# A weight slab moved between DMA queues, ahead of a transposing load, and second-layer weights in one load fewer

## The chip, the core and the metric

The kernel runs on one core of one Trainium2 chip. The metric is the device time of one execution in microseconds (us): the median of the runs, with the lowest and highest beside it. A core has five engines that each follow their own instruction stream: TensorE (PE in the profile, with its weight loads listed apart as PEld), VectorE (DVE), ScalarE (ACT), GpSimd (POOL) and SyncE (SP). DMA transfers are issued by an engine's queue; in this kernel only SP and ScalarE issue any. Each issue costs the issuing queue some time, and the data land later.

## The reference

The kernel computes two branches from one input x of 2048 rows and 512 columns in bf16 and mixes them by a gate for each row.

```python
g = _sigmoid((x * gate_w).sum(-1, keepdims=True))
# branch A: linear attention, 32 heads of 16
qkv = x @ wqkv                        # split into q, k, v for each head
pq, pk = q @ w_phi, k @ w_phi         # for each head
phi_q = concat([softmax(pq), softmax(-pq)])
phi_k = concat([softmax(pk), softmax(-pk)])
kv = einsum("bhsf,bhsd->bhfd", phi_k, v)
z  = einsum("bhsf->bhf", phi_k)
o  = (phi_q @ kv) / (phi_q @ z + 1e-6)
a  = o @ wo
# branch B: dense layer, relu, dense layer; 512 -> 1376 -> 512
b  = relu(x @ w1) @ w2
out = g * a + (1 - g) * b
```

## The kernel before

The work is written out by hand in one order for each engine. A small planner collects the operations of each engine in program order, with the events that each waits for, and emits them; it does not reorder. `p.early` places what follows ahead of the program's opening barrier, so that SP and ScalarE begin to issue loads at the start of the span.

Matrix products want x with its columns on the 128 partitions, so x is held transposed in XT: four blocks of 128 columns, 2048 rows each. Rows are taken in four chunks of 512. For chunk 0, the first two column blocks are loaded plainly (L158), transposed on TensorE against an identity (L236) and evicted by VectorE and ScalarE (L246, L248). The other two blocks of chunk 0 come by a transposing DMA straight from memory (L174, event `x0t`). Chunks 1 to 3 come whole by transposing DMAs (L187).

The first layer's weights lie in W1, one slab of 128 input rows for each column block of x. Each slab's first 1024 columns are one load, but for slab 0, which has two. The remaining columns of all slabs are a load of their own (L177). TensorE multiplies slab by slab for chunk 0 (L519): slab t is eight matmuls, one into each of the eight PSUM banks, which accumulate over the four slabs. Slab 2 and slab 3 need the blocks of x that the transposing DMA brings:

```python
XV = (("xva0", "xvc0", "xvd0"), ("xva1",), ("x0t",), ("x0t",))
...
after=["w10a" if t == 0 and u < 4 else f"w1{t}", *XV[t]] + (free[UB[u]] if t == 0 else []),
```

SP's queue issues in this order: the two plain x loads, slab 0 in two, slab 1, the transposing load of x (`x0t`), slab 3, the remaining columns, the per-head weights (L179), the value weights (L181), the query and key weights by two transposing loads (L184, `wqk0` and `wqk1`), and chunks 1, 2 and 3 of x (L187). Slab 2 is issued by ScalarE, after ScalarE's second eviction of transposed x (L537 calls L162).

After the slabs, TensorE does the last two units of chunk 0 (L271), the gate column (L223), two value tiles (L403), and then folds the per-head weights into the query and key weights (L305): four groups that read `wqk0`, one value tile, four groups that read `wqk1`. The leftover hidden columns of chunk 0 follow (L283), and then the main loop of 16 row tiles: query and key products (L327), exponentials (L347), sums, reciprocals and products for the softmaxes, transposes of the features by DMA on SP (L396), the sum over rows (L425), value tiles, and first-layer units of the later chunks (L271). In row tile 3, SP loads the second layer's weights into W2, in three loads of 4, 3 and 3 row blocks and one of the last 96 rows (L584, L587). After the loop come the attention outputs (L457), the second layer (L482), the output projection (L491), the mix (L505) and the stores (L510). The second layer waits for all loads of W2.

Of the kernel before, what the change touches and what calls it, by code (L numbers as in the profile page):

```python
# [68 lines left out]
def bass_gated_mix__linear_kernel_hedgehog__dense_activation_relu__prompt_kernel(  # L69
# [16 lines left out]
    DFF = B_w1.shape[1]  # L86
    P = 128
# [14 lines left out]
    KU = KT - 1  # L102
    NR = DFF - KU * P

    with ExitStack() as es:
# [45 lines left out]
        p = _Plan(["sp", "pool", "act", "dve", "pe"])  # L151
# [6 lines left out]
            p.dma("sp", lambda e: e.dma_start(  # L158
                out=XS[:, 2 * h:2 * h + 2, 0:2 * P], in_=xq[:, 2 * h:2 * h + 2, 0:2 * P]), f"x0{h}", ev=f"x0{h}")

        def loadw1(t, c0=0, c1=DFF, tag="", eng="sp"):
            p.dma(eng, lambda e: e.dma_start(  # L162
                out=W1[:, t, c0:c1], in_=B_w1[t * P:(t + 1) * P, c0:c1]), f"w1{t}{tag}", ev=f"w1{t}{tag}")

        for h in range(2):
# [3 lines left out]
        p.early("act")  # L169
        p.early("sp")  # L170
        loadw1(0, 0, 4 * P, "a")
        loadw1(0, 4 * P, 8 * P)
        loadw1(1, 0, 8 * P)
        p.dma("sp", lambda e: e.dma_start_transpose(  # L174
            out=XT[:, 2:4, 0:512], in_=x2[0:512, 2 * P:4 * P]), "x0t", ev="x0t")
        loadw1(3, 0, 8 * P)
# [51 lines left out]
        def warm(n, cols=512):  # L228
            for _ in range(n):
                p.op("pe", lambda e: e.matmul(PS[:, 4, 0:cols], ones[:, 0:P], ones[:, 0:cols], start=True, stop=True),  # L230
                     after=["one"])
# [9 lines left out]
        def xev(eng, nm, js, dts, bank):  # L241
            w = len(js) * P
            d = XT[:, dts[0]:dts[-1] + 1, js[0] * P:js[0] * P + w]
            s = PS[:, bank, 0:len(dts) * w].rearrange("p (t c) -> p t c", c=w)
            if eng == "dve":
                p.op("dve", lambda e: e.tensor_copy(d, s), after=[f"xt{nm}"], ev=f"xv{nm}")  # L246
            else:
                p.op("act", lambda e: e.activation(d, s, ACT.Copy), after=[f"xt{nm}"], ev=f"xv{nm}")  # L248
            free[bank] = [f"xv{nm}"]
# [150 lines left out]
        def vtile(m, eng="act", bank=2):  # L400
            b = m % VB
            for dt in range(NDT):
                p.op("pe", lambda e, dt=dt: e.matmul(  # L403
                    PS[:, bank, :], XT[:, dt, m * P:(m + 1) * P], WV[:, dt, :],
                    start=(dt == 0), stop=(dt == NDT - 1)),
                    after=((xready(m // 4) + ["wv"] + free[bank]) if dt == 0 else ()),
                    ev=(f"v{m}" if dt == NDT - 1 else None))
            dst, src = VS[:, b, :, 0:64], PS[:, bank, :].rearrange("p (g c) -> p g c", g=NG)
            after = [f"v{m}"] + ([f"kv{m - VB}"] if m >= VB else [])
            if eng == "dve":  # L410
                p.op("dve", lambda e: e.tensor_copy(dst, src), after=after, ev=f"cv{m}")
            else:
                p.op("act", lambda e: e.activation(dst, src, ACT.Copy), after=after, ev=f"cv{m}")  # L413
            free[bank] = [f"cv{m}"]

        def kv(m):
            b = m % NB
            vb = m % VB
            for g in range(NG):
                after = []  # L420
                if g == 0:
                    after = [f"pk{m}", f"cv{m}", f"one{vb}"]
                    if m == 0:
                        after += free[6] + free[7]
                p.op("pe", lambda e, g=g: e.matmul(  # L425
                    PS[:, 6 + g // 4, (g % 4) * GW:(g % 4) * GW + 65],
                    EB[:, b, 3, g * P:(g + 1) * P], VS[:, vb, g, 0:65],
                    start=(m == 0 and g % 4 == 0), stop=(m == NT - 1), skip_group_check=True),
                    after=after, ev=(f"kv{m}" if g == NG - 1 else None))
# [104 lines left out]
        xev("act", "c0", (2,), (0,), 2)  # L534
        xev("dve", "d0", (3,), (0,), 1)
        xev("act", "a1", (0, 1, 2, 3), (1,), 7)
        loadw1(2, 0, 8 * P, eng="act")  # L537
        warm(1, 384)
        slab(0)
        for b in range(VB):  # L540
# [27 lines left out]
        def unit(c, k):  # L568
            if k < 0:
                rest(c)  # L570
            else:
                hunit(c, k)

        for m in range(NT):
            atile(m)
            if m >= LAG:
                kv(m - LAG)
            if m + 3 < NT:
                vtile(m + 3)
            for u in mid[m]:  # L580
                unit(*u)
            if m == 3:
                for a, b in ((0, 4), (4, 7), (7, KU)):
                    p.dma("sp", lambda e, a=a, b=b: e.dma_start(  # L584
                        out=W2[:, a:b, :], in_=B_w2[a * P:b * P, :].rearrange("(j p) n -> p j n", p=P)),
                        "w2", ev=f"w2{a}")
                p.dma("sp", lambda e: e.dma_start(out=W2[0:NR, KU, :], in_=B_w2[KU * P:DFF, :]), "w2", ev="w2")  # L587
            if m == 5:
                for a in range(0, NDT, 2):
                    p.dma("sp", lambda e, a=a: e.dma_start(  # L590
                        out=WO[:, a:a + 2, :], in_=A_wo[a * P:(a + 2) * P, :].rearrange("(j p) n -> p j n", p=P)),
                        "wo", ev="wo" if a else None)
# [69 lines left out]
```

## Time and profile before

| | |
|---|---|
| median of 4 runs | 146.91 us (146.65 to 147.36) |
| profiled execution | 147.02 us |
| its span in the profile | 145.7 us |
| TensorE busy | 141.9 us, 953 instructions |
| VectorE, ScalarE, GpSimd busy | 91.6, 72.3, 52.1 us |
| slabs of chunk 0, L519 | 32 matmuls, 7.7 us busy |
| second layer, L482 | 182 matmuls, 40.2 us busy |

The span runs from the first to the last recorded instruction, and the device time has 1.3 us around it. An engine's queue is written with a q (SPq, ACTq); its rows are the issues of transfers, with the time that an issue took, and a list of issues gives how long each took from issue to landing. "PE", "PEld" and so on are the engines themselves. "L519" is line 519 of the kernel before. A row of the timeline has the start, the duration, the engine, the line, the operation, what it writes and reads, and how many instructions are merged in it; in brackets stands how long the engine was idle just before and for what. The chain is the work that ended last, followed back from the end: at each step to what released it. The names in the rows drop numbers, so W1 and W2 are both "W", and the tensor of transposed query and key weights is a part of PHQ. A row of busy time in a stretch has, after the stretch and its length, the busy time and count of PE, PEld, DVE, ACT and POOL, then the granted TensorE clock, the DMA share and the GB/s.

### The profile page before, as it was taken

To read this page: it belongs to the slowest core of one execution; us is meant where nothing else is said; L and a number is where in the kernel's file an instruction comes from. 1 tells how busy PE (TensorE), PEld (TensorE's weight loads), DVE (VectorE), ACT (ScalarE), POOL (GpSimd) and SP (SyncE) were. 2 spreads that over 40 slices of the span, in tenths; PEclk is the share of its full clock that TensorE was granted. 3 is DMA by queue.
4 is the path that set the end of the run, shared out by engine and by line. 5 is a ranking of instruction groups with operands and counts; after the bars stand their busy time and mean duration, and the time that the engine had idled before them with its cause. 6 is when DMAs were issued, how large, how long until landed. Compare 5 with 4: busy or idle time off the path is not lost.

```text
span 145.7 us, 2504 instructions
## 1 busy us (share of the span) xinstructions
PE 141.9 (97%) x953; PEld 72.4 (50%) x970; DVE 91.6 (63%) x156; ACT 72.3 (50%) x124; POOL 52.1 (36%) x62
## 2 busy tenths in 40 slices
PE   8989999999999999999999999999999999999994
PEld 3434754444456554545555555554444444444443
DVE  4318728777686878678698967664445555554342
ACT  4116567789778778797878862022211111111150
POOL 2022003778868678678869810200000000000000
DMA  5999995113359984325334431354242222322213
GB/s 149 252 309 193 242 173 122 37 35 76 72 102 369 139 181 86 71 58 110 76 72 90 90 72 40 73 108 127 60 104 73 72 72 62 86 72 74 72 44 107
DMA packets 46533, 16.12 MB, mean 111 GB/s; under 512 B 40408, under 2 KB 46136, under 8 KB 46520
## 3 DMA queue, kind: packets, MB, share of 16 engines
q1 hardware_dynamic: 46224, 15.65, 47.7%
q10 hardware_dynamic: 296, 0.30, 0.9%
q8 instruction: 8, 0.13, 0.3%
q14 instruction: 5, 0.04, 0.1%
HBM read 4.15 MB, written 2.10 MB: 43 GB/s over the span
## 4 chain that ended last, share of the span: by engine, by line
PE 94%; DMA 3%; issue 1%; DVE 1%; DVEq 0%; ACT 0%
PE PS L482 26%; PE PS L271 19%; PE PS L327 18%; PE PS L491 9%; PE PS L403 9%; DMA W<-in_B_w_dram 3%; PE PS L457 3%; PE PS L425 3%; PE PS L519 2%; PE PS L283 2%; PE PS L230 2%; PE PS L305 1%; PE PS L236 1%; DVE WQK L505 1%; DVE ONE L206 0%
## 5 line engine op out<-in xcount | busy, mean ns | idle before, releaser
L482 PE MATMUL PS<-W,HT 128*128 128x512 bf16 (+3 forms) x182 | 40.2, 366 | 0.3
L371 POOL TENSOR_TENSOR EB<-EB,SC 128x1024 bf16<-128x1024 bf16 x15 | 28.9, 1930 | 23.2 <-DVE SC L369 23.2
L347 ACT ACTIVATE EB<-PS 128x480 bf16<-128x480 f32 (+1 forms) x44 | 30.1, 756 | 14.2 <-PE PS L327 14.2
L496 ACT ACTIVATE TFA<-PS,GT 128x512 bf16<-128x512 f32 x16 | 11.0, 687 | 42.7 <-PE PS L491 42.7
L271 PE MATMUL PS<-XT,W 128*128 128x512 bf16 x123 | 30.1, 379 | 0.3
L327 PE MATMUL PS<-WQK,XT 128*128 128x480 bf16 x128 | 28.5, 366 | 0.0
L367 DVE TENSOR_REDUCE ZB<-EB 128x64 f32<-128x1024 bf16 x15 | 18.3, 1220 | 14.3 <-ACT EB L347 14.3
L505 DVE SCALAR_TENSOR_TENSOR WQK<-PS,OMG,TFA 128x512 bf16<-128x512 f32 (+2 forms) x17 | 12.2, 719 | 23.6 <-ACT TFA L496 22.4
L482 PEld LDWEIGHTS PS<-W,HT 128*128 128x128 bf16 (+1 forms) x187 | 17.0, 98 | 17.4
L257 ACT ACTIVATE HT<-PS 128x512 bf16<-128x512 f32 x35 | 20.3, 614 | 8.2 <-PE PS L519 6.7
L327 PEld LDWEIGHTS PS<-WQK,XT 128*128 128x128 bf16 x128 | 12.5, 98 | 13.6
L382 DVE TENSOR_REDUCE ZB<-EB 128x64 f32<-128x1024 bf16 x16 | 18.6, 1164 | 0.0
L271 PEld LDWEIGHTS PS<-XT,W 128*128 128x128 bf16 x128 | 12.0, 98 | 13.2
L391 POOL TENSOR_TENSOR EB<-EB,SC 128x512 bf16<-128x512 bf16 x16 | 16.9, 1059 | 1.3
L491 PE MATMUL PS<-WO,OT 128*128 128x512 bf16 x62 | 16.0, 378 | 0.1
L403 PE MATMUL PS<-WV,XT 128*128 128x512 bf16 x59 | 15.3, 378 | 0.3
L467 DVE TENSOR_TENSOR WQK<-PS,RDEN 128x512 bf16<-128x512 f32 x16 | 11.1, 691 | 0.6
L491 PEld LDWEIGHTS PS<-WO,OT 128*128 128x128 bf16 x64 | 6.1, 97 | 7.2
L413 ACT ACTIVATE VS<-PS 128x512 bf16<-128x512 f32 x14 | 8.5, 608 | 2.0 <-PE PS L403 2.0
L369 DVE RECIPROCAL SC<-ZB 128x64 f32<-128x64 f32 x16 | 8.8, 553 | 0.5
L519 PE MATMUL PS<-XT,W 128*128 128x512 bf16 x32 | 7.7, 395 | 0.6 <-DMA W<-in_B_w_dram 0.6
L403 PEld LDWEIGHTS PS<-WV,XT 128*128 128x128 bf16 x64 | 5.5, 97 | 4.8
(57 smaller groups left out, 84.4 us busy)
## 6 DMA issues: line engine op xcount, KB each, us to landing
out_dram<-WQK SPq DMA_DIRECT2D x15, 128.0 KB, 1.7
W<-in_B_w_dram SPq DMA_DIRECT2D x2, 384.0 KB, 4.7
W<-in_B_w_dram SPq DMA_DIRECT2D x2, 256.0 KB, 3.9
WV<-in_A_wqkv_dram SPq DMA_DIRECT2D x1, 512.0 KB, 5.9
W<-in_B_w_dram SPq DMA_DIRECT2D x1, 512.0 KB, 4.1
WO<-in_A_wo_dram SPq DMA_DIRECT2D x2, 256.0 KB, 3.5
W<-in_B_w_dram SPq DMA_DIRECT2D x1, 352.0 KB, 5.3
OT<-in_A_x_dram SPq DMA_DIRECT2D x2, 128.0 KB, 2.3
```

Source lines behind the costliest of these rows:

```text
L257: p.op("act", lambda e: e.activation(dst, src, ACT.Relu), after=[f"h{c}_{kt}"], ev=ev)
L271: p.op("pe", lambda e, t=t: e.matmul(PS[:, bank, :], W1[:, t, kt * P:(kt + 1) * P], XT[:, t, c * 512:(c + 1) * 512], start=(t == 0), stop= ...
L327: p.op("pe", lambda e, dt=dt, which=which: e.matmul(PS[:, which, 0:DE], XT[:, dt, m * P:(m + 1) * P], WQK[:, which, dt * DE:(dt + 1) * DE] ...
L347: p.op("act", lambda e: e.activation(dst, s_, ACT.Exp, scale=scale), after=[f"qk{m}"] + busy, ev=ev)
L367: p.op("dve", lambda e: e.tensor_reduce(zk, ek, AX.X, ALU.add), after=[emk, f"cst{b}"], ev=f"zk{m}")
L371: p.op("pool" if m < NT - 1 else "dve", lambda e: e.tensor_tensor(EB[:, b, 3, :].rearrange("p (g f) -> p g f", f=DH), EB[:, b, 2, :].rearr ...
L382: p.op("dve", lambda e: e.tensor_reduce(ZB[:, b, 0:64].rearrange("p (h s) -> p h s", s=2), bass.AP(tensor=EB, offset=base, ap=[[EBS, P], [ ...
L391: p.op("pool", lambda e: e.tensor_tensor(EB[:, b, 0, :].rearrange("p (h s f) -> p h s f", h=H, s=2)[:, :, 1, :], EB[:, b, 1, :].rearrange( ...
L403: p.op("pe", lambda e, dt=dt: e.matmul(PS[:, bank, :], XT[:, dt, m * P:(m + 1) * P], WV[:, dt, :], start=(dt == 0), stop=(dt == NDT - 1)), ...
L482: p.op("pe", lambda e, kt=kt, M=M: e.matmul(PS[:, bank, 0:n], HT[0:M, kt, m * P:(m + 1) * P], W2[0:M, kt, cs], start=(kt == 0), stop=(kt = ...
L491: p.op("pe", lambda e, t=t: e.matmul(PS[:, bank, :], OT[:, t, m * P:(m + 1) * P], WO[:, t, :], start=(t == 0), stop=(t == NDT - 1)), after ...
L505: p.op("dve", lambda e: e.scalar_tensor_tensor(out=OSB[:, ob, cs], in0=PS[:, bank, 0:n], scalar=OMG[:, m:m + 1], in1=TFA[:, m % 2, cs], op ...
```

## The change

The load of W1's slab 2 is taken from ScalarE's queue and put on SP's, behind slab 1 and ahead of the transposing load `x0t`. The helper `loadw1` loses its parameter for the engine. In row tile 3 the ten full row blocks of W2 come in two loads of five in place of three of 4, 3 and 3. Nothing else differs; the bytes loaded, the tiles and all computing instructions stay.

```diff
-        def loadw1(t, c0=0, c1=DFF, tag="", eng="sp"):
-            p.dma(eng, lambda e: e.dma_start(
+        def loadw1(t, c0=0, c1=DFF, tag=""):
+            p.dma("sp", lambda e: e.dma_start(
                 out=W1[:, t, c0:c1], in_=B_w1[t * P:(t + 1) * P, c0:c1]), f"w1{t}{tag}", ev=f"w1{t}{tag}")
...
         loadw1(0, 0, 4 * P, "a")
         loadw1(0, 4 * P, 8 * P)
-        loadw1(1, 0, 8 * P)
+        for t in (1, 2):
+            loadw1(t, 0, 8 * P)
         p.dma("sp", lambda e: e.dma_start_transpose(
             out=XT[:, 2:4, 0:512], in_=x2[0:512, 2 * P:4 * P]), "x0t", ev="x0t")
         loadw1(3, 0, 8 * P)
...
         xev("act", "a1", (0, 1, 2, 3), (1,), 7)
-        loadw1(2, 0, 8 * P, eng="act")
         warm(1, 384)
         slab(0)
...
             if m == 3:
-                for a, b in ((0, 4), (4, 7), (7, KU)):
+                for a, b in ((0, 5), (5, KU)):
                     p.dma("sp", lambda e, a=a, b=b: e.dma_start(
                         out=W2[:, a:b, :], in_=B_w2[a * P:b * P, :].rearrange("(j p) n -> p j n", p=P)),
                         "w2", ev=f"w2{a}")
```

## The prediction

> **What bounds the kernel now.** I read the busy shares first, then the chain that ended last.
>
> ```profile
> PE 141.9 (97%) x953; PEld 72.4 (50%) x970; DVE 91.6 (63%) x156; ACT 72.3 (50%) x124; POOL 52.1 (36%) x62
> ...
> PE 94%; DMA 3%; issue 1%; DVE 1%; DVEq 0%; ACT 0%
> ```
>
> TensorE is busy 97% of the span and carries 94% of the chain; only the other shares can be saved without removing a matmul. The 3% of DMA is one piece. The same chain in order of time, first 22 us:
>
> ```profile
> 3.57 0.02 issue
> 3.60 0.01 ACT XT L248
> 3.60 4.74 DMA W<-in_B_w_dram
> 8.34 0.05 issue
> 8.39 3.63 PE PS L519 x16
> ```
>
> At 3.60 ScalarE has evicted the last transposed x block (L248) and issues a weight load: slab 2, the only W1 load on its queue. It lands at 8.34, and at 8.39 TensorE begins slabs 2 and 3 (16 matmuls). The timeline (start, duration) of the three queues, with the two weight loads on PEld that matter later:
>
> ```profile
> 2.55 1.33 SPq L174 DMA_TRANSPOSE XT<-in_A_x_dram  x1
> ...
> 3.60 0.37 ACTq L162 DMA_DIRECT2D W<-in_B_w_dram  x1
> ...
> 3.78 4.03 PE L519 MATMUL PS<-XT,W 128*128 128x512 bf16 x16
> ...
> 3.94 0.57 SPq L162 DMA_DIRECT2D W<-in_B_w_dram  x1
> ...
> 8.39 3.63 PE L519 MATMUL PS<-XT,W 128*128 128x512 bf16 x16 [0.57 <-DMA W<-in_B_w_dram]
> ...
> 15.12 1.05 PEld L305 LDWEIGHTS PS<-Wbd,PHQ 128*128 128x128 bf16 x16
> ...
> 16.82 1.05 PEld L305 LDWEIGHTS PS<-Wbd,PHQ 128*128 128x128 bf16 x16
> ```
>
> The reader is to see two things. Slabs 0 and 1 end at 3.78+4.03 = 7.81, slab 2 begins at 8.39. And the stall is more than the 0.57 printed: 16 matmuls in 3.63 with a single one of 0.38 (0.379 in the line's own view) means a step of (3.63-0.38)/15 = 0.216. The last of slab 1 started at 7.81-0.38 = 7.43, so the next could start at 7.65. It started at 8.39: **0.74 us** are lost.
>
> What lands when: issue rows of the stretches 2.0-2.5, 2.5-3, 3.5-3.9, 3.9-4.5, 6-7 and 13-14 (KB of each, us from issue to landing).
>
> ```profile
> W<-in_B_w_dram SPq DMA_DIRECT2D x1, 256.0 KB, 3.1
> ...
> XT<-in_A_x_dram SPq DMA_TRANSPOSE x1, 3.6
> ...
> W<-in_B_w_dram ACTq DMA_DIRECT2D x1, 256.0 KB, 4.7
> ...
> W<-in_B_w_dram SPq DMA_DIRECT2D x1, 256.0 KB, 4.6
> ...
> PHQ<-in_A_wqkv_dram SPq DMA_TRANSPOSE x1, 8.0
> ...
> PHQ<-in_A_wqkv_dram SPq DMA_TRANSPOSE x1, 4.7
> ```
>
> With the issue times: slab 1 lands at 2.08+3.1 = 5.2, the transposed x at 2.55+3.6 = 6.15, slab 2 at 8.3, slab 3 at 3.94+4.6 = 8.5, the two halves of the transposed query and key weights at 6.12+8.0 = 14.1 and 11.38+4.7 = 16.1. The other rows give: W1's remaining columns 4.54+5.3 = 9.8, per-head weights 10.0, value weights 5.57+5.9 = 11.5.
>
> **The change, part by part.**
>
> *Slab 2 leaves ScalarE's queue.* It removes 0.37 us of issue there. ScalarE's next work is the first relu, at 10.54, waiting 6.3 us for TensorE: nothing gained.
>
> *Slab 2 goes on SP at 2.55 in place of 3.60.* Nearest row: slab 1, same size, same queue, just ahead: 3.1 us, so it lands at 5.65 at the earliest; slab 1 landed 0.9 after the load ahead of it (5.2 against 4.3), so 5.2+0.9 = 6.1 if it must follow slab 1's data; with the 4.7 of the ScalarE load 7.25 at the latest. I take 6.1. All three are before 7.65, so this wait ends.
>
> *The transposing load is moved behind it.* Its issue starts later by one SP issue, 0.43 plus 0.04 between two = 0.47, thus at 3.02. Slab 2 also needs it, so it is late next. Low bound, the issue shift alone: 6.15+0.47 = 6.6. High bound: the 4.7 that the slowest load of this size took, 3.02+4.7 = 7.7. Between: it follows slab 2's data, which takes 0.9: 6.15+0.9 = 7.05. [...] I take 7.05, 0.6 of cover left.
>
> *All that SP issues later is 0.47 later at issue:* slab 3, the remaining columns, per-head weights, value weights, two transposing weight loads, three x chunks. TensorE will want each 0.74 earlier. Landing before, against the new need: slab 3 8.5 against 8.39+8*0.216-0.74 = 9.38; remaining columns 9.8 against 11.64-0.74 = 10.9; value weights 11.5 against 13.58-0.74 = 12.84; first transposed half 14.1 against 15.12-0.74 = 14.38; **second half 16.1 against 16.82-0.74 = 16.08**; chunk 1 (13.88+4.6 = 18.5) against 20.84-0.74 = 20.1. The second half has no slack, so what its landing does decides how much of 0.74 stays. Do bytes or issues set it? The issue of the first half took 5.21 us, that of the second, equal half 2.46: SP was held some 2.75 us by what was queued ahead, so 0.47 of later issue before it disappears there. And the bytes are the same:
>
> ```profile
> 7.00:8.00 1.00, 0.81 (x4) 0.20 (x2) 0.37 (x2) 0.00 (x0) 0.00 (x0) 1.00 1.00 341
> ...
> 9.00:10.00 1.00, 1.00 (x6) 0.48 (x5) 0.00 (x0) 0.00 (x0) 0.00 (x0) 1.00 1.06 344
> ```
>
> In these rows the last columns are the DMA share and GB/s: with two queues at work (7-8) 341, with SP's alone (9-10) 344. Whatever ran on ScalarE's queue took its time from SP's. So the landing of the second half stays near 16.1: bounds are 0.3 earlier (in 6-7 us only 233 GB/s flowed, a dip which might close) and 0.47 later. I take 16.1, stall 0.02 to 0.05.
>
> *Second-layer weights in two loads and the rest.*
>
> ```profile
> 41.37 1.66 SPq L584 DMA_DIRECT2D W<-in_B_w_dram  x3
> ...
> W<-in_B_w_dram SPq DMA_DIRECT2D x2, 384.0 KB, 4.7
> ...
> 88.07 2.38 PE PS L482 x11
> ```
>
> One load of three goes, about 0.5 us of SP issue (1.66/3 = 0.55). [...] SP's transposes behind them start up to 0.5 us earlier; the first is only read by L457 at 87.82. [...] I count 0.
>
> *The rest of the span.* From 8.39 to the end the chain is TensorE with gaps of at most 0.3 us, set by engines fed from TensorE itself, so they shift with it.
>
> **Sum:** profiled execution 147.02 (span 145.7, 1.3 around it); -0.74 for the stall, +0.04 at the second transposed half, 0 for the rest: 146.3. It lies 0.11 above the median 146.91, so on the median's scale 146.91-0.70 = **146.2**.
>
> **The rivals.** A difference below 0.3% (0.44 us: faster below 146.47, slower above 147.35) can hardly be told from no change.
>
> *A, forecast (0.62):* 146.2, own range 145.9 to 146.5, from no second stall (-0.74) to a stall of 0.3, with 0.15 for the scatter of 146.65 to 147.36 seen before.
>
> *B, the gain is half given back at L305 (0.15).* SP's stream is late by the full 0.47 and TensorE waits that long for the second transposed half: 146.91-0.74+0.49 = 146.66. For it: zero slack there. Against: SP was held 2.75 us at this very place.
>
> *C, a wait takes the place of the one removed (0.12).* The transposed x gates slab 2. The gain is all gone if it lands at 8.34, 5.3 us after its issue; it took 3.6. For it: the load behind a transpose took 4.6 to 4.7, so a switch between the two kinds may cost time. Against: 0.6 of cover at my estimate, and 7.7 as high bound costs 0.1. Time 146.9.
>
> *D, slower (0.11).* ScalarE's queue did give its 256 KB beside SP's stream; on SP they push every later load by 0.9, and the issue by 0.47 more. The second transposed half then lands at 16.1+1.37 = 17.45 where TensorE wants it at 16.08: 146.91-0.74+1.37 = 147.54. It decides from a landing of 16.08+0.74+0.44 = 17.3 on. Against: 341 and 344 GB/s.
>
> **How the numbers follow.** Faster: nine tenths of A, a fifth of B: 0.59. Slower: most of D and a little of C: 0.12. The same: 0.29. The range 145.9 to 147.0 holds A, B and C but for their tails, and leaves out D and a lower tail, together under 0.2.
>
> **What would show it.** Right: slab 2's first matmul at about 7.65, no DMA piece of several us left in the chain, slab 2 landed near 6.1, x near 7.05, L305's second group at 16.1 with no wait or a short one, all later groups 0.7 earlier, W2 without effect. Wrong: slab 2 waits for XT's transposing load (C); a DMA wait appears ahead of L305, or of L519's slab 3 (B, D); or the early gap closes and the end stays, which would mean that some later wait is tied to a load and not to TensorE.

## The result, and the profile after

Over many executions the changed kernel took 146.95 us (median of 43, 146.3 to 147.78) and the kernel before 147.25 us (median of 64, 146.65 to 150.11). The ratio is **0.997, with a 95% interval of 0.9959 to 0.9982**: 0.44 us faster (0.27 to 0.60); the medians differ by 0.30. The forecast, 146.2 against 146.91, was a gain of 0.71 and a ratio of 0.9952. The direction was right; the gain was put too high. Of the 0.75 us between the forecast of 146.2 and the 146.95 measured, 0.34 is the kernel before itself, whose median is 147.25 here and was 146.91 in the four runs known to the forecast. The ratios leave out executions that were disturbed (a granted clock of 0.988 or 0.989 in place of 1.000, or a time far above the fastest), and as the profiles of e2, e4 and e16 were taken in such executions, no explanation rests on them.

The page of the changed kernel, busy shares and chain (lines 174 to 536 of the kernel before stand one higher here: L519 is now L520, L305 is L306, and so on):

```profile
PE 142.0 (98%) x953; PEld 72.5 (50%) x970; DVE 91.6 (63%) x156; ACT 72.3 (50%) x124; POOL 52.1 (36%) x62
...
PE 97%; issue 1%; DVE 1%; DVEq 0%
```

The chain's 3% of DMA is gone. In order of time, its first part:

```profile
3.59 0.32 PE PS L231
3.91 7.63 PE PS L520 x32
11.54 0.65 PE PS L272 x3
```

All four slabs are one piece of 32 matmuls. The wait for slab 2 no longer exists. But the unit behind the slabs, L272, starts at 11.38 in the timeline against 11.85 before, **0.47 us earlier and not 0.74**, and the last matmul is 0.48 earlier (143.09 against 143.57). So what was lost was lost in the first 11 us. Weight loads on PEld, start and duration, first of the changed kernel:

```profile
3.78 0.14 PEld L520 LDWEIGHTS PS<-XT,W 128*128 128x128 bf16 x2 [0.35 <-DMA W<-in_B_w_dram]
4.19 0.15 PEld L520 LDWEIGHTS PS<-XT,W 128*128 128x128 bf16 x1 [0.28 <-issue]
4.62 0.15 PEld L520 LDWEIGHTS PS<-XT,W 128*128 128x128 bf16 x1 [0.28 <-issue]
5.04 6.00 PEld L520 LDWEIGHTS PS<-XT,W 128*128 128x128 bf16 x28 [0.28 <-issue]
...
16.47 0.92 PEld L306 LDWEIGHTS PS<-Wbd,PHQ 128*128 128x128 bf16 x16 [0.24 <-DMA PHQ<-in_A_wqkv_dram]
```

and then of the kernel before:

```profile
4.16 0.15 PEld L519 LDWEIGHTS PS<-XT,W 128*128 128x128 bf16 x1 [0.28 <-issue]
4.59 2.73 PEld L519 LDWEIGHTS PS<-XT,W 128*128 128x128 bf16 x13 [0.28 <-issue]
```

A row that stands alone, 0.43 behind the one before it, belongs to a matmul at half the later rate (0.427 us a step in place of 0.216). Before, TensorE left that slow stretch at about 4.7; in this execution at about 5.2 (both worked out from the one step that is part slow, part fast). That one more slow step costs 0.24 us, and slab 0 began 0.03 later (3.81 against 3.78): 0.74-0.24-0.03 = 0.47.

The last row is the second transposed half. Its weight load waited 0.24 us for the landing. TensorE's matmuls themselves did not wait: the load began 0.21 us ahead of them in the kernel before (16.82 and 17.03) and 0.09 ahead here (16.47 and 16.56), so the wait used up what was to spare. With 0.47 us of gain the kernel stands almost at this landing. The issue rows of the stretches 3-3.4, 6.5-7 and 12-14:

```profile
XT<-in_A_x_dram SPq DMA_TRANSPOSE x1, 4.5
...
PHQ<-in_A_wqkv_dram SPq DMA_TRANSPOSE x1, 7.6
...
PHQ<-in_A_wqkv_dram SPq DMA_TRANSPOSE x1, 5.2
```

x lands at 3.02+4.5 = 7.5, the first half at 6.60+7.6 = 14.2, the second at 11.20+5.2 = 16.4.

### The profile page after: what moved, and what is told of

It is laid out like the page before. It is cut to its first block, busy times and chain, and to the rows that moved or that the text cites. A ratio compares the mean times of both kernels' runs of the same rounds, so it can differ in the third digit from the quotient of the medians.

```text
span 145.3 us, 2503 instructions
## 1 busy us (share of the span) xinstructions
PE 142.0 (98%) x953; PEld 72.5 (50%) x970; DVE 91.6 (63%) x156; ACT 72.3 (50%) x124; POOL 52.1 (36%) x62
## 4 chain that ended last, share of the span: by engine, by line
PE 97%; issue 1%; DVE 1%; DVEq 0%
PE PS L483 26%; PE PS L272 19%; PE PS L328 18%; PE PS L492 9%; PE PS L404 9%; PE PS L520 5%; PE PS L458 3%; PE PS L426 3%; PE PS L284 2%; PE PS L231 2%; PE PS L306 1%; PE PS L237 1%; DVE WQK L506 1%; DVE ONE L207 0%; DVEq L647 0%
## 5 line engine op out<-in xcount | busy, mean ns | idle before, releaser
L348 ACT ACTIVATE EB<-PS 128x480 bf16<-128x480 f32 (+1 forms) x44 | 30.1, 756 | 14.2 <-PE PS L328 14.2
L272 PE MATMUL PS<-XT,W 128*128 128x512 bf16 x123 | 30.1, 379 | 0.3
L483 PEld LDWEIGHTS PS<-W,HT 128*128 128x128 bf16 (+1 forms) x187 | 17.0, 98 | 17.4
L272 PEld LDWEIGHTS PS<-XT,W 128*128 128x128 bf16 x128 | 12.0, 98 | 13.2
L468 DVE TENSOR_TENSOR WQK<-PS,RDEN 128x512 bf16<-128x512 f32 x16 | 11.1, 691 | 0.6
L458 PEld LDWEIGHTS PS<-KVNZ,PHQ 128*128 128x128 bf16 x128 | 6.1, 97 | 3.6
```

Of the source, the lines that this page charges most:

```text
L272: p.op("pe", lambda e, t=t: e.matmul(PS[:, bank, :], W1[:, t, kt * P:(kt + 1) * P], XT[:, t, c * 512:(c + 1) * 512], start=(t == 0), stop= ...
L348: p.op("act", lambda e: e.activation(dst, s_, ACT.Exp, scale=scale), after=[f"qk{m}"] + busy, ev=ev)
L483: p.op("pe", lambda e, kt=kt, M=M: e.matmul(PS[:, bank, 0:n], HT[0:M, kt, m * P:(m + 1) * P], W2[0:M, kt, cs], start=(kt == 0), stop=(kt = ...
```

## The experiments

**Theory R**: the moment at which TensorE goes over to the fast rate (from 0.427 us a step to 0.216) differs between executions; before, a late one disappeared in the wait for slab 2, and now it reaches the end. **Theory L**: the landing of the second transposed half caps the gain when TensorE starts fast. **Theory W**: the merged second-layer loads cost time. **Theory C** came later, for the transposing load beside ScalarE's copy. The runs were taken in five batches (a "call" in the expectations), each with its own runs of the kernel before. Its median differed between them (147.23 to 148.13), so kernels are compared inside a batch. The expectations, as they stood before each run, are printed ahead of the results.

### Each part of the change alone

e1 has the slab moved and W2 in three loads; e2 has W2 in two loads and the slab where it was.

```diff
# e1, on the changed kernel
-                for a, b in ((0, 5), (5, KU)):
+                for a, b in ((0, 4), (4, 7), (7, KU)):
# e2, on the kernel before: the reverse
```

> The changed kernel with the second-layer weights again in three loads; only slab 2 moved. Theory R (half rate): the changed profile lost 0.24 of the 0.74 us because TensorE ran one more of slab 0's matmuls at 0.427 us instead of 0.216; the second-layer loads play no part, so the ratio to before is 0.997, as for the whole change, and slab 2 starts right behind slab 1. Theory W (the merged second-layer loads cost time): ratio near 0.995 (-0.7 us), the forecast of the first step alone.

> The kernel before with the second-layer weights in two loads; slab 2 stays on ScalarE's queue. Theories R and L (landing of the second transposed half): ratio 1.000. Theory W: 1.001 to 1.002 (+0.15 to +0.3 us).

e1: 146.88 us, ratio 0.9924 (0.9904 to 0.9944). e2: ratio 1.0018 (0.9991 to 1.0044). The slab's move alone makes the kernel faster. The times do not decide on theory W: e1 is nearer to W's number than to R's, and e2's 1.0018 is what W expects, with an interval that holds 1.000 as well. The traces decide it. From the start of the second L306 group, long before these loads, to the end of the device time there are 130.02 to 130.05 us with two merged loads (five profiles of the changed kernel), and 129.99 (before), 130.01 (e11 below) and 130.02 us (e1) with three. W's number, 0.15 to 0.3 us, is not there: at most 0.06.

### The rate at the start

e8 and e10 are the changed kernel again, for more profiles. e5 and e6 are the two kernels without the four matmuls on ones that keep TensorE busy from 0.4 us on and whose results nobody reads:

```diff
# e5 on the changed kernel, e6 on the kernel before
-        warm(4)
         p.early("pe")
```

> The changed kernel once more, for a second profile and the pair of times beside the others. Theory R: the number of slab matmuls at 0.427 us is a matter of the execution, two to five; the start of the first unit behind the slabs (L272) moves by 0.21 us for each; in an execution with two only, it starts at 11.15. Theory L: then TensorE waits for the second transposed half ahead of the second L306 group, by the difference of its landing to 16.1. If the count is always four, the gain is 0.45 to 0.5 us in each profile.

> The changed kernel beside the others of this call. Theory R: where TensorE starts slab 0 at the fast rate, slab 2 starts by 7.65 and the second L306 group waits; where four or more matmuls are slow, slab 2 starts at 7.9 or later and it waits little. Either way the second L306 group starts between 16.5 and 17.2.

> The changed kernel without the four matmuls on ones at the start (L231), which compute nothing that is used. TensorE then starts at about 2.4 us in place of 0.4 and should go over to the fast rate some 2 us later, with four to five more slab matmuls at 0.427 us. Theory R: nothing hides that, the time rises by 0.8 to 1.1 us over the changed kernel, to a ratio to before of 1.002 to 1.004. Rival (what precedes slab 2 has no bearing, 0.74 us are saved whatever the rate): the same rise here, but then the same rise in the kernel before without those matmuls too.

> The kernel before without the four matmuls on ones at the start. Theory R: the wait for slab 2 ends at 8.34 us whatever TensorE's rate before; of 0.8 to 1.1 us of later slab 0 and 1, 0.74 is absorbed, so the time rises by only 0 to 0.4 us (ratio 1.000 to 1.003), and the two kernels without those matmuls differ by less than 0.2 us. Rival: ratio 1.005 to 1.007, and the changed one stays 0.44 us or more below it.

In one batch: before 148.13 us, changed 146.69 (e8, ratio 0.9916, 0.9883 to 0.9948), changed without those matmuls 147.66 (e5, 0.9986, 0.9958 to 1.0014), before without them 148.02 (e6, 1.0012, 0.9991 to 1.0033). **The longer slow start costs the changed kernel 0.97 us and the kernel before nothing that can be told** (-0.11). The move is then worth 0.36 us in place of 1.44, though e8 has only six runs. Theory R had the rise of 0.8 to 1.1 and the absorption right; the ratio of e5 (1.002 to 1.004) and a distance below 0.2 were missed, since the kernel before itself was at 148.13 in this batch. The rival, a kernel before that rises to 1.005 or more, is out. The chains show it, e5 first:

```profile
3.59 0.32 PE PS L231
3.91 9.17 PE PS L520 x32
13.08 1.51 PE PS L272 x7
```

```profile
4.37 0.01 issue
4.38 8.67 PE PS L519 x32
13.05 1.51 PE PS L271 x7
```

The second fence is e6, with slab 2 on ScalarE's queue: its four slabs, too, are one piece, with no wait for slab 2. Both kernels reach the unit behind the slabs at 13.1, and both spans are 146.8. That these two agree so closely is partly chance: e5 has 11 slow steps, and e6 has 8 but began slab 0 0.57 us later, at 4.38.

In e10 six steps of slab 0 are slow. Its PEld rows end the slow stretch at 6.3, so slab 2 starts only at 8.44, and there is no wait after it (ratio 0.995, 0.9928 to 0.9972):

```profile
5.87 0.15 PEld L520 LDWEIGHTS PS<-XT,W 128*128 128x128 bf16 x1 [0.28 <-issue]
6.29 5.28 PEld L520 LDWEIGHTS PS<-XT,W 128*128 128x128 bf16 x25 [0.27 <-issue]
```

In e8 no step is slow. Slab 2 starts at 7.65, the time of the forecast, but by luck: slab 0 waited 0.60 us for its own weights and started at 4.19 in place of 3.78. Then the chain turns to SP's queue and to the second half:

```profile
6.60 4.62 SPq L185
11.22 0.04 issue
11.26 5.39 DMA PHQ<-in_A_wqkv_dram
16.65 0.05 issue
16.70 1.01 PE PS L306 x16
```

The count of slow steps was expected at two to five and ran from none to six. All profiles of the changed kernel and e1, whose first 40 us are the same program (times in us; the third column is issue plus time to landing of the second half):

| profile | slow stretch ends | second half lands | its L306 group starts | TensorE waited for it |
|---|---|---|---|---|
| changed | 5.2 | 16.4 | 16.56 | 0 |
| e8 | before slab 0 | 16.65 | 16.70 | 0.41 |
| e10 | 6.3 | 16.4 | 17.08 | 0 |
| e15 | 4.9 | 16.65 | 16.69 | 0.28 |
| e18 | before slab 0 | 17.2 | 17.25 | 0.50 |
| e1 | before slab 0 | 17.13 | 17.18 | 1.05 |

The wait is the start of this group less the start of the first L306 group less the 1.70 us between them when nothing waits. The longest of these waits, in e1:

```profile
17.18 1.01 PE L306 MATMUL PS<-Wbd,PHQ 128*128 128x120 bf16 x16 [0.87 <-DMA PHQ<-in_A_wqkv_dram]
```

From this group on hardly anything differs: the last matmul starts 126.53 or 126.54 us after it in the first profiles of the changed kernel and the kernel before. The device time of each of the six executions, and of the two of the kernel before, where the group starts at 17.03 and (e11, below) 17.75, is the group's start plus 129.99 to 130.05 us, so where this group starts decides the time.

### The landing of the second transposed half

Variants that read it later, and one (e17) that lands it earlier.

```diff
# e3, on the changed kernel (e14 the same)
+        rest(0)
         for i in range(4, 8):
             pre(i)
-        rest(0)
# e14 besides: other PSUM banks for that group
-            bank = (0, 1, 6, 7)[i % 4]
+            bank = (0, 1, 6, 7, 6, 7, 2, 1)[i]
# e9, on the changed kernel; e12 the same on the kernel before
         vtile(2, "dve")
+        vtile(3, "act", nextbank())
         for i in range(4, 8):
...
-            if m + 3 < NT:
+            if 0 < m and m + 3 < NT:
                 vtile(m + 3)
# e13, on e9
         vtile(3, "act", nextbank())
+        rot[0] += 2
...
-        mid = [[(1, 0), (1, 1)], [(1, 2), (1, 3)], [(1, 4), (1, 5)], [(1, 6), (1, 7)], [(1, 8), (1, 9)], [(2, 0)],
+        mid = [[(1, 0), (1, 1), (1, 2)], [(1, 3), (1, 4)], [(1, 5), (1, 6)], [(1, 7), (1, 8)], [(1, 9)], [(2, 0)],
# e17, on the changed kernel
-            out=WV[:, :, :], in_=A_wqkv[:, 2 * D:3 * D].rearrange("(j p) n -> p j n", p=P)), "wv", ev="wv")
+            out=WV[:, 0:2, :], in_=A_wqkv[0:2 * P, 2 * D:3 * D].rearrange("(j p) n -> p j n", p=P)), "wv", ev="wv")
...
+        p.op("pool", lambda e: e.memset(WV[:, 2:4, :], 0.0), ev="wvz")
... (the value tiles then wait for "wvz" too)
```

> The changed kernel with the leftover columns of chunk 0 (16 matmuls, 0.69 us) computed ahead of the second group of four that folds per-head weights, so that the second transposed half is read 0.69 us later. Theory L (its landing at 16.4 us caps the gain): the wait of 0.24 us ahead of that group goes, and the time falls by up to 0.25 us below the changed kernel, ratio to before 0.9955. Theory R: TensorE's starts did not move for that wait in the changed profile, so the ratio stays 0.997, unless the reordering delays evictions ahead of the first row tile (then up to +0.3 us).

> The changed kernel with the fourth value tile (four matmuls, 0.86 us, all it needs is there) computed ahead of the second group of L306 instead of in row tile 0. The second transposed half is then wanted 0.86 us later, up to 16.9. Theory L (its landing at 16.4 to 17.1 us caps the gain whenever TensorE starts fast): no wait or one under 0.2 us ahead of that group, and the time falls by 0.2 to 0.5 us below the changed kernel. Rival (the landing only mirrors a TensorE that is late for its own reasons): the time stays with the changed kernel's within 0.1 us.

> The kernel before with the same reordering of the fourth value tile. Theory L: TensorE comes late to the second L306 group there (16.82 against a landing of 16.1), so that nothing is waiting to be saved, ratio 1.000 (0.997 to 1.001). Rival (the reordering is worth something by itself, the slab's queue or not): a gain as large as in the changed kernel, 0.2 to 0.5 us.

> The changed kernel with the fourth value tile ahead of the second L306 group, the rotation of PSUM banks kept as it was, and the units of chunk 1 moved one row tile forward, so that ScalarE has as much time between row tiles as before. Theory L: no wait at the second L306 group (wanted at 16.9 or later), 0.2 to 0.5 us faster than the changed kernel in the same call, ratio to it 0.997 to 0.999, unless chunk 1 of x, then wanted at 20.2, lands later (20.6 in one profile) and takes it back. Rival (the wait is only a mirror of TensorE's own lateness): same as the changed kernel within 0.1 us.

> The changed kernel with the leftover columns ahead of the second L306 group, as in the earlier run, and with other PSUM banks for that group, so that the first row tile does not wait for an eviction of the bank that it needs (0.29 us in that run). Theory L: the group is wanted at up to 16.7, the wait goes in executions that start fast, 0.2 to 0.4 us faster than the changed kernel in the same call. Rival: the same within 0.1 us.

> The changed kernel, beside these two. By all runs so far the second L306 group starts between 16.5 and 17.2, and the ratio to before is 0.991 to 0.997.

> The changed kernel that loads only the first half of the value weights (256 KB less ahead of the transposed query and key weights on SP's queue) and sets the other half to zero on GpSimd; the values are thus computed from half of x's columns, the amount of computing is the same. The second transposed half should land 0.7 us earlier, at 15.3 to 16. Theory L: no wait ahead of the second L306 group, the median falls by 0.2 to 0.4 us below the changed kernel's, ratio to it 0.997 to 0.999. Rival (another wait or the slow start decides, not this landing): the same as the changed kernel within 0.1 us.

> The changed kernel beside it: ratio to before 0.991 to 0.997, and by theory R and L the second L306 group starts between 16.5 and 17.2.

e3: 146.74 us, ratio 0.9898 (0.9854 to 0.9942), in the batch of e1 (146.88), six runs. Its execution started fast, and no wait for the half is left. But the half landed at 15.93 there, and TensorE would have come to it at 14.21+1.70 = 15.91 without the reordering, so this profile had hardly a wait to remove. And 0.29 us came back as a wait for an eviction into WQK (L311):

```profile
16.77 0.22 PE PS L306 x4
16.99 0.02 issue
17.01 0.67 DVE WQK L311
17.68 0.05 issue
17.73 1.79 PE PS L328 x8
```

e9 (1.0005, 0.9982 to 1.0028; the changed kernel e10 in the same batch 0.995) and e12 (1.0073, 1.0047 to 1.0098) say nothing on L. The reordering shifts the rotation of PSUM banks, and the first second-layer product waits for the last relu, 0.53 us in the timelines of both (this is e9's):

```profile
88.23 2.10 PE L483 MATMUL PS<-W,HT 128*128 128x512 bf16 x9 [0.53 <-ACT HT L258]
```

In e13 below, with the rotation put right, it has no room: from the start of the second L306 group in its chain (18.07) to the end of its 147.23 us are 129.16 us, 0.70 less than in e10 (147.10-17.24 = 129.86), and the value tile moved ahead of the group is 0.86. e9's chain also met the next load in SP's queue, chunk 1 of x, which landed only at 20.64:

```profile
13.64 6.99 DMA XT<-in_A_x_dram
20.64 0.05 issue
20.68 1.90 PE PS L272 x8
```

e13, with rotation and units put right, e14 and the changed kernel e15 beside them came out alike: 146.79, 146.80 and 146.79 us (0.9956, 0.9938 to 0.9975; 0.9965, 0.9946 to 0.9983; 0.9968, 0.9951 to 0.9986). The gain of 0.2 to 0.5 us that L promised is not there. The profiles of e13 and e14 had slow starts (slab 2 at 8.41 and 8.61). In their chains TensorE goes without a wait into the second L306 group, at 18.07 and 18.10; without the 0.86 and 0.69 us computed ahead of it, it would have come there at about 17.2 and 17.4, by when the half had landed in all six executions of the table (17.2 at the latest). So there was hardly a wait to remove.

e17 computes the values from half of x's columns only and so loads 256 KB less ahead of the half. It lands at 10.22+5.3 = 15.5, as expected. 146.64 us against 147.03 for the changed kernel beside it (e18), 0.39 less; ratios to before 0.9952 (0.9927 to 0.9976) and 0.9975 (0.9959 to 0.9990). The size is L's, but the intervals overlap, and e17's profile, with a slow start (slab 2 at 8.72), has no wait that the earlier landing could have removed. In e18, which started fast, the waits of TensorE show that it meets one late load after another:

```profile
PEld PS L306 <- DMA PHQ<-in_A_wqkv_dram: 1.4, 2, 0.8
PEld PS L520 <- DMA W<-in_B_w_dram: 0.9, 2, 0.5
...
PE PS L306 <- DMA PHQ<-in_A_wqkv_dram: 0.3, 1, 0.3
PE PS L520 <- DMA XT<-in_A_x_dram: 0.2, 1, 0.2
```

So the landing as a limit is shown in the traces of four of the six executions. That removing it alone pays in time is not shown: e17's median points that way within the noise, e13 and e14 do not. No variant that computes the whole output was shown to be faster than the changed kernel.

### The queue, the place and the issue time

```diff
# e4, on the kernel before: slab 2 on ScalarE's queue, but as its first weight load
         p.early("sp")
+        loadw1(2, 0, 8 * P, eng="act")
...
-        loadw1(2, 0, 8 * P, eng="act")
# e7, on the changed kernel: slab 2 behind the transposing load
-        for t in (1, 2):
-            loadw1(t, 0, 8 * P)
+        loadw1(1, 0, 8 * P)
         p.dma("sp", lambda e: e.dma_start_transpose(
             out=XT[:, 2:4, 0:512], in_=x2[0:512, 2 * P:4 * P]), "x0t", ev="x0t")
-        loadw1(3, 0, 8 * P)
+        for t in (2, 3):
+            loadw1(t, 0, 8 * P)
# e16, on the kernel before: slab 3 ahead of the transposing load on SP
+        loadw1(3, 0, 8 * P)
         p.dma("sp", lambda e: e.dma_start_transpose(
             out=XT[:, 2:4, 0:512], in_=x2[0:512, 2 * P:4 * P]), "x0t", ev="x0t")
-        loadw1(3, 0, 8 * P)
```

e11 is the kernel before once more, for a second profile.

> The kernel before, with slab 2 still on ScalarE's queue but issued as its first weight load, some 2.6 us earlier than at 3.60. If the wait was due to the late issue and not to the queue, slab 2 lands before 7.65 and the time falls as in the changed kernel, ratio 0.997; if the queue itself made it late, it lands after 7.65 and the ratio stays 1.000. If it takes the place of slab 0's and slab 1's data, TensorE waits at slab 0 or 1, up to 0.7 us there, and part of the gain goes: 0.998 to 1.002.

> The changed kernel with slab 2 behind the transposing load of x on SP's queue, ahead of slab 3. If only the queue and the issue time matter, x lands at 6.2 and slab 2 at about 7.1, both before 7.65, and the ratio is that of the changed kernel, 0.997. If slab 2 lands after 7.65 (it was issued last but one before the wait), TensorE waits there, and the ratio lies between 0.997 and 1.000. It tells whether the place ahead of the transposing load matters.

> The kernel before, for a profile of it on the same chip as the others. If the larger distance of the two kernels here (ratio 0.992, against 0.997 over many chips) comes from slab 2 on ScalarE's queue, it lands later than 8.34 here, by up to 1 us, and TensorE's wait ahead of slab 2 is longer than 0.74. If it comes from elsewhere, it lands at 8.3 and a wait or a slow stretch shows at another place.

> The kernel before, slab 2 on ScalarE's queue at 3.6, with slab 3's load ahead of the transposing load of x on SP. Theory C (a copy from the other queue and a transposing load in flight together slow each other): slab 2 lands some 3 us after its issue in place of 4.7 to 6.8, by 7.0, and x lands by about 7.6, so that slab 2 starts at 7.7 to 8.0 and the ratio is below 0.998. Rival (the load from ScalarE's queue is late by itself): slab 2 lands at 8.3 or later again, ratio 1.000 or above.

e4: 1.0023 (0.9990 to 1.0055). An early issue on ScalarE's queue does not give the gain; why is not settled. In its one profile, on which by the above nothing can rest, slab 2 landed at 4.40 and was not late, but slab 0's first part landed only at 4.62 (1.19+2.5 = 3.7 in the first profile of the changed kernel, 1.19+2.1 = 3.3 in that of the kernel before).

e7: 147.24 us, 0.9941 (0.9921 to 0.9961), in the batch of e8 (146.69): SP's queue behind the transposing load gives part of the gain. In its profile slab 2 landed at 8.05, 0.4 too late for 7.65, but five slow steps kept TensorE from it until 8.22. What TensorE waited for was the second half, which landed at 17.47 (0.66 us).

e11: ratio 0.9999 (0.9966 to 1.0032), and its chain shows where the kernel before loses more than in the first profile:

```profile
3.54 5.51 DMA W<-in_B_w_dram
9.05 0.05 issue
9.10 3.63 PE PS L519 x16
```

Slab 2 landed at 9.05, not at 8.34, and TensorE stood still for 1.20 us, though it left its slow stretch at 5.1, much as the changed kernel in its profile. The transposing load of x, in flight at the same time, took longer as well:

```profile
XT<-in_A_x_dram SPq DMA_TRANSPOSE x1, 5.6
```

With slab 2 in flight from ScalarE's queue it took 3.6 (the first profile), 5.6 (e11), 5.6 (e6) and 6.5 us (e12), and slab 2 4.7, 5.5, 5.2 and 6.75. With slab 2 on SP's own queue it took 3.8 to 4.5 in thirteen profiles. Differences between the batches do not explain it: beside e6 the transposing load took 3.8 (e7), 4.2 (e5) and 4.2 us (e8), beside e11 and e12 4.5 us (e9 and e10). e16 was to part the two; it came out slower (1.0109, 1.0044 to 1.0173, from three executions), against theory C's number, but by its program order the transposing load and ScalarE's copy are still issued close to each other (3.02 and 3.62), so it does not decide. That the two slow each other is the reading that fits these durations. The nearest test is e7, which has slab 2 behind the transposing load too, but on SP's queue, issued 0.33 us later and ahead of slab 3; there slab 2 took 4.1 us and the transposing load 3.8. It is one profile, and the first profile of the kernel before has 3.6.

## Why the prediction was off, step by step

- **The wait for slab 2 ends.** Right: slab 2 landed at 6.2 to 6.5 in all six profiles (forecast 6.1), its landing holds nothing up, and the chain has no DMA piece from ScalarE. But the sign that the prediction gave for rivals B and D, a DMA wait ahead of L305 (here L306), is there in four of the six.
- **"The last of slab 1 started at 7.43, so the next could start at 7.65", and thus 0.74 us.** This is the first step that failed. It is right for the execution that was profiled, but it takes TensorE's time over slabs 0 and 1 as fixed. The slow stretch ends anywhere from before slab 0 to 6.3 us, and slab 2 started between 7.50 and 8.44. The wait used to hide this; e5 and e6 show it in time, 0.97 us against nothing that can be told. In the profile after, it is 0.27 of the missing gain.
- **"I take 16.1, stall 0.02 to 0.05" for the second transposed half.** The second step that failed, in its size. The forecast saw zero slack there and counted with the landing of one execution. The half landed at 16.4 to 17.2, and TensorE waited 0.28, 0.41, 0.50 and 1.05 us in four of six executions. Rival B, which gives half of the gain back at this place, describes this in size. Its reason, SP's stream late by the full 0.47, fits only in part: the half's issue came at 11.1 to 11.3 in three of the six and at 11.5, 11.7 and 12.15 in the others, against 11.38, and its landing took 4.9 to 5.6 us in place of 4.7. Nor is it shown that the change made the landing late. With slab 2 on ScalarE's queue the half landed at 16.8 in e11 and 17.0 in e6, later than the changed kernel beside them (16.4 in e10, 16.65 in e8), and in e3, with the changed kernel's loads, it landed at 15.9. The 16.1 was an early landing, and the forecast took it for the rule. What sets the landing in one execution stays open.
- **How the two add up.** They stand in for each other: a slow start leaves little or no wait at the half, a fast one runs into it. On average of the six, the first L306 group started at 14.83, 0.24 later than 15.33-0.74 = 14.59, and the wait ahead of the second was 0.37 us where the forecast had 0.04. The second group started at 16.56 to 17.25, 16.91 on average; the forecast had 17.03-0.74+0.04 = 16.33.
- **x lands at 7.05.** Late: 7.2 to 7.5, since it came 1.05 to 1.3 us behind slab 2 and not 0.9. The cover against 7.65 was 0.1 to 0.4 and not 0.6; x held up slab 2 by 0.40 us in e18 and by about 0.1 in e1, where it landed at 3.02+4.3 = 7.3 and slab 2's first weight load came at 7.47 against 5.66+8*0.216 = 7.39 (rival C, in small).
- **341 and 344 GB/s, so ScalarE's queue takes its time from SP's.** The sum was read rightly, and rival D did not come about. But the sum hides that the transposing load beside ScalarE's copy took up to 2.9 us longer than in the first profile, so that the kernel before can lose more than 0.74: 1.20 in e11. This, with few runs in some batches, fits that comparisons of the same pair of kernels gave 0.9916 to 0.9975; it was not isolated.
- **Second-layer loads at nothing, the rest of the span unmoved.** Right: the end keeps its distance to the second L306 group within 0.06 us, with two loads or three. The loads have long landed when they are read: in the kernel before the last of them was issued at 43.07 and landed 5.5 us later, at 48.6, and the first second-layer product stands at 88.07 in the chain, 39 us behind; in the changed kernel the last landed at 42.08+6.2 = 48.3.

## What to carry to other kernels

A wait that ends with a landing can hide what varies ahead of it, as here a longer slow start cost nothing that can be told with the wait and 0.97 us without it; when the wait is taken away, that variation reaches the end, so the gain can be less than the wait of one profile. Before counting the whole wait as gain, look at more than one profile for the spread of the busy stretch before it and of the next landing behind it. A slack of zero against a landing that varies by 0.8 us was a wait in four of six executions here.

## What was not expected of the hardware

TensorE's slow stretch ended less than 3.4 us after its first matmul at 0.38 us in e1, and 5.9 us after it in e10; the two programs are the same up to row tile 3. No run shows what sets this moment. The steps in e10 were 0.427 us before it and 0.216 after it. The clock column of the profile's rows does not show it. This row of the changed kernel (stretch, length, PE, PEld, DVE, ACT and POOL busy, clock, DMA share, GB/s) has 1.00 while every step is slow:

```profile
4.00:5.00 1.00, 1.00 (x3) 0.29 (x2) 0.26 (x2) 0.23 (x1) 0.00 (x0) 1.00 0.87 300
```

In these views only the spacing of equal matmuls, 0.427 us against 0.216, gives it away.
